# Column rings for the input and output buffers of a grouped 1x1 convolution, and a loop over 64 groups in place of 48

## The chip, the cores and the metric

The kernel runs on one core of one Trainium2 chip. The metric is the device time of one execution in microseconds (us). Where a ratio is given with an interval, it is the record's: the mean time of one kernel's fast runs over the mean of the other's in the same rounds. For the experiments these rounds leave out the profiled run, so it is not quite the ratio of the medians that are quoted.

## The reference, cut to what matters

```python
# x: (1, 512, 512, 192) bf16, w: (1, 1, 4, 48, 48) bf16; k = 1, G = 4, Cg = 48, pad = 0
xg = x.reshape(B, H, W, G, Cg)
out = jnp.einsum('bhwgc,gcd->bhwgd', xg, w[0, 0])      # 1x1 convolution in 4 groups
return out.reshape(B, H, W, C)
```

That is 262,144 pixels with 192 channels. Reading x takes 100.7 MB and writing the output takes 100.7 MB. There is little arithmetic for each byte.

## The kernel before

A "column" is 128 pixels, one on each of the 128 partitions, 384 bytes on each. There are 2,048 columns. They are moved in pieces: 4, 4, 8, 16 columns, then 62 pieces of 32, then 16, 8, 4, 4. A piece of 32 is one DMA of 1.5 MiB, in which each of the 128 partitions has one packet of 12,288 bytes. PE works on "groups" of four columns: six transposes, an eviction by DVE from PSUM to SBUF, six matmuls, and an eviction by ACT to the output buffer. In every third group DVE takes half of that last eviction ("shared" groups).

SP issues the loads, ACT issues the stores. In the kernel before, every piece, however small, holds one of six whole buffers of 32 columns, on either side:

```python
PPC = 32; NBI = 6; NBO = 6; RING = 6
x_sb = [... [128, PPC * C] ... for i in range(NBI)]
o_sb = [... [128, PPC * C] ... for i in range(NBO)]
body = NBI * PPC // 4                    # 48 groups in PE's hardware loop

def shared(g):
    return g % 3 == 1 and g < NG - 3

# SP
for n in range(n_chunks):
    if n >= NBI:
        wq.wait(t_done, chunk_g1[n - NBI])          # transposes of the piece six back
    b = n % NBI
    sp.dma_start(x_sb[b][:, 0:sizes[n] * C], rows_view(xf, n)).then_inc(ld_sem[b], 16)
# ACT, DVE: before the first write into an output buffer
def wait_out_free(wq, n):
    wq.wait(st_sem[n % NBO], 16 * (n // NBO))
# ... (PE, evictions: cut)
```

## Time and profile before

| | before |
|---|---|
| time, median of the first 3 runs | 493.58 us |
| profiled span | 492.4 us |
| bytes moved / mean rate over the span | 201.56 MB / 409 GB/s |
| rate in the middle of the run | 427 to 430 GB/s |
| busy: PE / DVE / ACT | 415 / 358 / 346 us |

These are lines of the page of the kernel before: the busy time of PE, then the span in 40 slices (PE's busy tenths, the DMA engines' mean busy tenths, the rate in GB/s), the queue that brings in instructions in 16 KiB packets, and the chain of waits that ended last, by engine and by line.

```profile
PE 415.0 (84%) x6154; PEld 389.1 (79%) x6154; DVE 358.1 (73%) x683; ACT 345.6 (70%) x513; POOL 1.3 (0%) x8
...
PE   5999999998888888888889888888888888888953
...
DMA  8999999999999999999999999999999999999663
GB/s 294 414 418 425 427 427 429 430 429 429 430 429 429 429 428 427 427 429 427 428 430 429 429 430 430 429 430 427 428 427 429 428 429 429 429 429 427 279 253 143
...
q8 instruction: 7, 0.11, 0.1%
...
DMA 71%; PE 24%; ACT 3%; issue 1%; ACTq 1%; SPq 0%
DMA x_sb<-in_x_dram 71%; PE o_ps L207 13%; PE xT_ps L184 10%; ACT o_sb L274 3%; ACTq L258 1%; SPq L155 0%; SPq L150 0%; ACTq L47 0%
```

DMA is full from the second slice to the 37th, at about 429 GB/s, and no compute engine is. The chain consists mostly of loads of x. So far this looks like a kernel at the bandwidth limit. But the last three slices are far from full, and that calls for a closer look.

The waits of the kernel before (who waited for whom: us in total, times, longest) and then the wait of the load queue on SP:

```profile
DVE xT_sb L242 <- PE xT_ps L184: 109.7, 243, 4.0
ACT o_sb L274 <- PE o_ps L207: 101.6, 169, 7.2
...
PE xT_ps L184 <- DMA x_sb<-in_x_dram: 58.3, 54, 3.2
...
PE o_ps L207 <- ACT o_sb L274: 10.1, 45, 0.4
```

```profile
SPq L155 <- PE xT_ps L184: 427.2, 64, 7.6
```

PE is starved by loads. The queue on SP always waits for transposes: each freed buffer gets its next load at once. No wait for a store is listed. The DMA issues, with the median time from issue to landing:

```profile
x_sb<-in_x_dram SPq DMA_DIRECT2D x62, 1536.0 KB, 39.2
out_dram<-o_sb ACTq DMA_DIRECT2D x62, 1536.0 KB, 31.0
```

A load of 1.5 MiB lands 39.2 us after its issue, though one such piece passes every 7.6 us. About five of the six buffers are thus queued loads. Stretches of the run, with the busy time of each engine, then the granted clock, the DMA engines' share and GB/s:

```profile
core 0: us, PE busy (x) PEld busy (x) DVE busy (x) ACT busy (x) POOL busy (x), PEclk, DMA share, GB/s
135.00:440.00 305.00, 257.58 (x3845) 240.78 (x3843) 224.26 (x428) 215.89 (x322) 0.00 (x0) 1.00 1.01 429
456.00:462.00 6.00, 5.59 (x85) 5.11 (x82) 4.95 (x10) 4.96 (x8) 0.00 (x0) 1.00 0.88 359
462.00:468.00 6.00, 5.06 (x78) 4.85 (x78) 4.34 (x9) 4.00 (x7) 0.00 (x0) 1.00 0.42 178
468.00:474.00 6.00, 4.89 (x75) 4.67 (x76) 4.00 (x8) 4.71 (x7) 0.00 (x0) 1.00 0.59 243
474.00:478.00 4.00, 1.45 (x24) 1.25 (x21) 1.51 (x3) 1.18 (x2) 0.00 (x0) 1.00 0.72 301
...
480.00:482.00 2.00, 0.07 (x1) 0.08 (x2) 0.00 (x0) 0.00 (x0) 0.00 (x0) 0.50 0.06 26
482.00:484.00 2.00, 2.00 (x17) 1.97 (x18) 0.90 (x2) 0.36 (x1) 0.00 (x0) 0.50 0.06 25
```

The share is 1.01 until late and then 0.42 to 0.72, although loads are still outstanding: PE gets its last load at 481.9 us. From 480 to 484 us the share is 0.06, and one engine of 16 would be 0.0625: a single DMA engine is at work. It had no pause earlier: from 60 to 452 us the times of the packets, summed from the packed trace, add up to at least 16.1 engines in every half microsecond (over 16 because packets overlap a little), so no engine stood still. The trace also shows how one engine comes to be left over. Each load and store raises its semaphore 16 times, and the trace has the time of each increment (the load queue holds 1,136 packets of 4 bytes for its 71 DMAs, 16 for each). I read each increment as one engine's share done; the end agrees with that: one store has 15 increments by 472.5 us and the last at 484.2, and from 480 to 484 us one engine is at work. These are the 16 increments, in us from the start, of one load late in the run:

```
406.6 407.0 407.2 407.7 407.8 408.1 408.1 408.1 408.1 408.5 408.9 408.9 408.9 409.5 413.4 424.6
```

Fourteen engines finish their share within 3 us, one is 4 us later, and one is 15 us behind the last of the fourteen. The distance of the last increment from the median is 16.5 us here; for a load at 20 us it was 1.7 us, and it grows steadily. One engine is slower than the others, and this load is not complete until that engine's share is there, at 424.6 us. Of all packets of 12,288 bytes 93% took at most 0.465 us and 5% took 0.475 us or more.

### The profile page before, as it was taken

Reading aid. Unit: us, or ns where it says so; the run is one execution under the profiler, and the core shown is the slowest. Engines: PE = TensorE matmul, PEld = TensorE weight load, DVE = VectorE, ACT = ScalarE, POOL = GpSimd, SP = SyncE. Lnnn points to the kernel's source line nnn. Section 1 sums busy time; section 2 is a strip of 40 time slices with the busy share of each in tenths; the row PEclk is TensorE's granted clock in tenths of the full one; section 3 lists DMA queues with packets and bytes.
Section 4 is the critical chain, followed back from the end, with each engine's and each line's share of the span. In section 5 each row is a group of like instructions: output and inputs, shape, how many; then the busy total and the mean of one; then the engine's idle time right before and its main releaser. Section 6 shows DMA issues by size and latency. Waiting matters only on the chain.

```text
span 492.4 us, 14343 instructions
## 1 busy us (share of the span) xinstructions
PE 415.0 (84%) x6154; PEld 389.1 (79%) x6154; DVE 358.1 (73%) x683; ACT 345.6 (70%) x513; POOL 1.3 (0%) x8
## 2 busy tenths in 40 slices
PE   5999999998888888888889888888888888888953
PEld 5899999887877877878778778787787787877852
DVE  3888888876777777777778777777677777777750
ACT  2788888876766777667767676776776766766752
POOL 1000000000000000000000000000000000000000
PEclk9999999999999999999999999999999999999996
DMA  8999999999999999999999999999999999999663
GB/s 294 414 418 425 427 427 429 430 429 429 430 429 429 429 428 427 427 429 427 428 430 429 429 430 430 429 430 427 428 427 429 428 429 429 429 429 427 279 253 143
DMA packets 20386, 201.56 MB, mean 409 GB/s; under 512 B 2448, under 2 KB 3472, under 8 KB 4496
## 3 DMA queue, kind: packets, MB, share of 16 engines
q1 hardware_dynamic: 10288, 100.69, 48.5%
q10 hardware_dynamic: 10080, 100.67, 48.3%
q8 instruction: 7, 0.11, 0.1%
q14 instruction: 11, 0.09, 0.0%
HBM read 100.68 MB, written 100.66 MB: 409 GB/s over the span
## 4 chain that ended last, share of the span: by engine, by line
DMA 71%; PE 24%; ACT 3%; issue 1%; ACTq 1%; SPq 0%
DMA x_sb<-in_x_dram 71%; PE o_ps L207 13%; PE xT_ps L184 10%; ACT o_sb L274 3%; ACTq L258 1%; SPq L155 0%; SPq L150 0%; ACTq L47 0%
## 5 line engine op out<-in xcount | busy, mean ns | idle before, releaser
L242 DVE COPY xT_sb<-xT_ps 128x768 bf16<-128x768 bf16 x512 | 283.8, 555 | 114.8 <-PE xT_ps L184 109.7
L274 ACT CAST o_sb<-o_ps 128x768 bf16<-128x768 f32 x342 | 267.0, 799 | 107.9 <-PE o_ps L207 101.6
L184 PE MATMUL xT_ps<-ident,x_sb 128*128 128x128 bf16 x3072 | 257.2, 220 | 58.3 <-DMA x_sb<-in_x_dram 58.3
L207 PE MATMUL o_ps<-wt,xT_sb 128*128 128x144 bf16 (+1 forms) x3072 | 297.4, 233 | 10.4 <-ACT o_sb L274 10.1
L184 PEld LDWEIGHTS xT_ps<-ident,x_sb 128*128 128x128 bf16 x3072 | 195.0, 98 | 70.0 <-DMA x_sb<-in_x_dram 68.9
L207 PEld LDWEIGHTS o_ps<-wt,xT_sb 128*128 128x128 bf16 x3072 | 211.5, 98 | 24.5 <-issue 17.7
L271 ACT CAST o_sb<-o_ps 128x384 bf16<-128x384 f32 x170 | 81.6, 480 | 33.3 <-PE o_ps L207 24.0
L248 DVE CAST o_sb<-o_ps 128x384 bf16<-128x384 f32 x170 | 94.2, 554 | 8.1 <-PE o_ps L207 7.0
L237 DVE CAST wt<-o_ps 128x480 bf16<-128x480 f32 x1 | 0.7, 657 | 3.2 <-PE o_ps L167 3.2
L167 PE MATMUL o_ps<-w_sb,esel 48*128 48x48 bf16 x10 | 0.6, 209 | 2.6 <-DMA w_sb<-in_w_dram 2.6
L167 PEld LDWEIGHTS o_ps<-w_sb,esel 48*128 48x128 bf16 x10 | 0.4, 111 | 2.5 <-POOL esel L139 2.5
L274 ACT ACT_TABLE_LOAD x1 | 1.3, 1283 | 0.8 <-PEq L298 0.8
L139 POOL TENSOR_SCALAR_AFFINE_SELECT esel<-esel 48x272 bf16<-48x272 bf16 x1 | 0.4, 406 | 0.0
L136 POOL MEMSET esel<- 48x272 bf16 x1 | 0.3, 318 | 0.3 <-POOLq L298 0.3
L143 POOL TENSOR_SCALAR_AFFINE_SELECT ident<-ident 128x128 bf16<-128x128 bf16 x1 | 0.3, 285 | 0.0
L137 POOL MEMSET ident<- 128x128 bf16 x1 | 0.2, 198 | 0.0
L298 POOL MEMSET const-bfloat16-1.0<- 128x1 bf16 x1 | 0.1, 102 | 0.0
L298 POOL MEMSET const-uint8-127<- 128x1 uint8 x1 | 0.1, 102 | 0.0
L298 POOL MEMSET const-float32-0.0<- 128x1 f32 x1 | 0.1, 98 | 0.3 <-issue 0.3
L298 POOL MEMSET const-float32-1.0<- 128x1 f32 x1 | 0.1, 98 | 0.0
## 6 DMA issues: line engine op xcount, KB each, us to landing
x_sb<-in_x_dram SPq DMA_DIRECT2D x62, 1536.0 KB, 39.2
out_dram<-o_sb ACTq DMA_DIRECT2D x62, 1536.0 KB, 31.0
x_sb<-in_x_dram SPq DMA_DIRECT2D x2, 768.0 KB, 22.1
out_dram<-o_sb ACTq DMA_DIRECT2D x2, 768.0 KB, 11.7
x_sb<-in_x_dram SPq DMA_DIRECT2D x4, 192.0 KB, 15.5
x_sb<-in_x_dram SPq DMA_DIRECT2D x2, 384.0 KB, 19.8
out_dram<-o_sb ACTq DMA_DIRECT2D x4, 192.0 KB, 6.9
out_dram<-o_sb ACTq DMA_DIRECT2D x2, 384.0 KB, 10.2
```

Source lines behind the costliest of these rows:

```text
L136: gp.memset(esel[:], 1.0).then_inc(p0_sem, 1)
L139: gp.affine_select(out=esel[:], in_=esel[:], pattern=[[-1, ECOLS]], compare_op=AluOpType.is_equal, fill=0.0, base=ESHIFT, channel_multipli ...
L167: last = pe.matmul(o_ps[:, NOB - 1, col:col + CG], lhsT=esel[:, s0:s0 + 128], rhs=w_sb[:, g, :], start=True, stop=True, skip_group_check=True)
L184: ins.append(pe.transpose(xT_ps[:, g % NXP, j * 128:(j + 1) * 128], xb[:, col:col + 128], ident[:]))
L207: ins.append(pe.matmul(o_ps[:, v % NOB, c0_:c1_], lhsT=xs[:, j * 128:(j + 1) * 128], rhs=wt[:, WOFF[tc]:WOFF[tc] + (c1_ - c0_)], start=(tc ...
L237: dve.tensor_copy(wt[:], o_ps[:, NOB - 1, 0:WCOLS]).then_inc(wc_sem, 1)
L242: dve.tensor_copy(xT_sb[g % NXP][:], xT_ps[:, g % NXP, 0:2 * UC]).then_inc(e1_sem[g % RING], 1)
L248: dve.tensor_copy(o_sb[n % NBO][:, u * UC:(u + 1) * UC], o_ps[:, v % NOB, 0:UC]).then_inc(d2_sem[g // 3 % 2], 1)
L258: act.dma_start(rows_view(of, n), o_sb[b][:, 0:sizes[n] * C]).then_inc(st_sem[b], 16)
L271: ins = act.copy(ob[:, u * UC:(u + 1) * UC], o_ps[:, v % NOB, 0:UC])
L274: ins = act.copy(dst, o_ps[:, v % NOB:v % NOB + 2, 0:UC])
L298: nc = _bacc.Bacc("TRN2", target_bir_lowering=False, num_devices=1)
```

## The change

The intent is to use the buffers fully. Input and output become one ring of 256 columns each. A piece takes only its own columns, and a load waits only until the transposes have passed the columns that it overwrites. PE's hardware loop then covers a ring, 64 groups in place of 48, and so that this divides evenly, every fourth group is shared in place of every third.

```diff
-PPC = 32
-NBI = 6
-NBO = 6
-RING = 6
+BIG = 32
+RCOLS = 256
+RING = 8
 ...
-    body = NBI * PPC // 4
+    body = RCOLS // 4
 ...
     def shared(g):
-        return g % 3 == 1 and g < NG - 3
+        return g % 4 == 1 and g < NG - 3
 ...
-        x_sb = [... [128, PPC * C] ... for i in range(NBI)]
-        o_sb = [... [128, PPC * C] ... for i in range(NBO)]
+        x_sb = ... [128, RCOLS * C] ...
+        o_sb = ... [128, RCOLS * C] ...
 ...
-        def wait_out_free(wq, n):
-            wq.wait(st_sem[n % NBO], 16 * (n // NBO))
+        def wait_out_free(wq, g):
+            if g >= body:
+                p = store_at[g - body]
+                wq.wait(st_sem[p.key], st_val[p])
 ...
-            for n in range(n_chunks):
-                if n >= NBI:
-                    wq.wait(t_done, chunk_g1[n - NBI])
-                b = n % NBI
-                sp.dma_start(x_sb[b][:, 0:sizes[n] * C], rows_view(xf, n)).then_inc(ld_sem[b], 16)
+            for p in loads:
+                wq.wait(t_done, p.g1 - body)
+                sp.dma_start(ring_view(x_sb, p), rows_view(xf, p)).then_inc(ld_sem[p.key], 16)
 ... (semaphores by piece, indices into the rings: cut)
```

More of the change, by code (lines that the diff above doesn't have):

```diff
@@ L47, in wait, with __init__, plan_pieces @@
         self.eng.wait_ge(sem, val)
-def plan_chunks(npix):
-    assert npix % 512 == 0, "the pixel count must be a multiple of 512"
-    cols = npix // 128
-    head, tail = list(HEAD), list(TAIL)
-    if cols < sum(head) + sum(tail) + PPC:
-        head, tail = [], []
-    mid = cols - sum(head) - sum(tail)
-    first = len(head)
-    full = mid // PPC
-    sizes = head + [PPC] * full
-    if mid % PPC:
-        sizes.append(mid % PPC)
-    return sizes + tail, first, full
+class Piece:
+    def __init__(self, col, size, key):
+        self.col, self.size, self.key = col, size, key
+        self.g0, self.g1 = col // 4, (col + size) // 4
+def plan_pieces(cols, head, tail):
+    sizes = list(head) if cols >= sum(head) + sum(tail) else []
+    last = list(tail) if sizes else []
+    mid = cols - sum(sizes) - sum(last)
+    pieces, c = [], 0
+    for s in sizes + [BIG] * (mid // BIG) + ([mid % BIG] if mid % BIG else []) + last:
+        whole = s == BIG and c % BIG == 0
+        pieces.append(Piece(c, s, ("big", c // BIG % (RCOLS // BIG)) if whole else ("own", len(pieces))))
+        c += s
+    return pieces
 def bass_standalone__grouped__vision_kernel(nc, x, w, out):
@@ L68, in bass_standalone__grouped__vision_kernel @@
     npix = B * H * W_
-    sizes, first_full, n_full = plan_chunks(npix)
-    n_chunks = len(sizes)
+    cols = npix // 128
+    assert npix % 512 == 0, "the pixel count must be a multiple of 512"
+    NG = cols // 4
+    loads = plan_pieces(cols, HEAD, TAIL)
+    stores = plan_pieces(cols, HEAD, TAIL)
+    load_of = {p.g0: p for p in loads}
+    store_at = {g: p for p in stores for g in range(p.g0, p.g1)}
+    store_end = {p.g1 - 1: p for p in stores}
     xf = x.rearrange("b h w c -> (b h w) c")
@@ L75, in bass_standalone__grouped__vision_kernel @@
     wv = w.rearrange("a b g c d -> c (a b g) d")
-    col0, groups, chunk_g0, chunk_g1, c0 = [], [], [], [], 0
-    for n, s in enumerate(sizes):
-        col0.append(c0)
-        c0 += s
-        chunk_g0.append(len(groups))
-        groups += [(n, lg) for lg in range(s // 4)]
-        chunk_g1.append(len(groups))
-    NG = len(groups)
-    body = NBI * PPC // 4
-    assert body % 12 == 0
-    loop_g0 = chunk_g0[first_full]
-    reps = max(0, (n_full * PPC // 4 - LOOK) // body)
+    body = RCOLS // 4
+    assert body % RING == 0 and BIG % 4 == 0 and RCOLS % BIG == 0
+    bigs = [p for p in loads if p.key[0] == "big"]
+    loop_g0 = bigs[0].g0 if bigs else 0
+    reps = max(0, (sum(p.size for p in bigs) // 4 - LOOK) // body)
     loop_g1 = loop_g0 + reps * body
     def shared(g):
-        return g % 3 == 1 and g < NG - 3
+        return g % 4 == 1 and g < NG - 3
     dve_prog = [("wcopy", 0)]
@@ L101, in bass_standalone__grouped__vision_kernel, with rows_view, ring_view @@
             dve_prog.append(("ev2", h))
-    def rows_view(ap, n):
-        s = sizes[n]
-        return ap[128 * col0[n]:128 * (col0[n] + s), :].rearrange("(p i) c -> p (i c)", p=128)
+    def rows_view(ap, p):
+        return ap[128 * p.col:128 * (p.col + p.size), :].rearrange("(p i) c -> p (i c)", p=128)
+    def ring_view(t, p):
+        at = p.col % RCOLS
+        assert at + p.size <= RCOLS
+        return t[:, at * C:(at + p.size) * C]
     with ExitStack() as es:
         block = es.enter_context(nc.Block())
-        x_sb = [es.enter_context(nc.sbuf_tensor(f"x_sb{i}", [128, PPC * C], BF16)) for i in range(NBI)]
-        o_sb = [es.enter_context(nc.sbuf_tensor(f"o_sb{i}", [128, PPC * C], BF16)) for i in range(NBO)]
+        x_sb = es.enter_context(nc.sbuf_tensor("x_sb", [128, RCOLS * C], BF16))
+        o_sb = es.enter_context(nc.sbuf_tensor("o_sb", [128, RCOLS * C], BF16))
         xT_sb = [es.enter_context(nc.sbuf_tensor(f"xT_sb{i}", [128, 2 * UC], BF16)) for i in range(NXP)]
@@ L120, in sem @@
             return es.enter_context(nc.semaphore(name))
-        ld_sem = [sem(f"ld{i}") for i in range(NBI)]
-        st_sem = [sem(f"st{i}") for i in range(NBO)]
+        ld_sem = {k: sem(f"ld_{k[0]}{k[1]}") for k in dict.fromkeys(p.key for p in loads)}
+        st_sem = {k: sem(f"st_{k[0]}{k[1]}") for k in dict.fromkeys(p.key for p in stores)}
+        st_val, seen = {}, {}
+        for p in stores:
+            seen[p.key] = seen.get(p.key, 0) + 16
+            st_val[p] = seen[p.key]
         w_sem, id_sem, e_sem, wb_sem, wc_sem = (sem(s) for s in ("w_sem", "id_sem", "e_sem", "wb_sem", "wc_sem"))
@@ L171, in transposes @@
             def transposes(g):
-                n, lg = groups[g]
                 if g == 0:
                     pe.wait_ge(id_sem, 1)
-                if lg == 0:
-                    pe.wait_ge(ld_sem[n % NBI], 16)
-                xb = x_sb[n % NBI]
+                p = load_of.get(g)
+                if p:
+                    pe.wait_ge(ld_sem[p.key], 16)
                 ins = []
                 for ul in range(2):
-                    u = lg * 2 + ul
+                    u = g % body * 2 + ul
                     for tc in range(3):
@@ L184, in transposes @@
                         ins.append(pe.transpose(xT_ps[:, g % NXP, j * 128:(j + 1) * 128],
-                                                xb[:, col:col + 128], ident[:]))
-                if lg == 0:
-                    ins[1].then_inc(ld_sem[n % NBI], -16)
+                                                x_sb[:, col:col + 128], ident[:]))
+                if p:
+                    ins[1].then_inc(ld_sem[p.key], -16)
                 ins[-1].then_inc(t_done, 1)
@@ L197, in matmuls @@
                     if shared(g - 2):
-                        waited.append(d2_sem[(g - 2) // 3 % 2])
+                        waited.append(d2_sem[(g - 2) // 4 % 2])
                 for s in waited:
@@ L238, in _ @@
                     continue
-                n, lg = groups[g]
                 if op == "ev1":
@@ L243, in _ @@
                 else:
-                    wait_out_free(wq, n)
+                    wait_out_free(wq, g)
                     wq.wait(mm_done, g + 1)
-                    u = lg * 2 + 1
+                    u = g % body * 2 + 1
                     v = 2 * g + 1
-                    dve.tensor_copy(o_sb[n % NBO][:, u * UC:(u + 1) * UC],
-                                    o_ps[:, v % NOB, 0:UC]).then_inc(d2_sem[g // 3 % 2], 1)
+                    dve.tensor_copy(o_sb[:, u * UC:(u + 1) * UC],
+                                    o_ps[:, v % NOB, 0:UC]).then_inc(d2_sem[g // 4 % 2], 1)
         @block.scalar
@@ L254, in _, with store @@
             pending = []
-            def store(n):
-                b = n % NBO
-                act.dma_start(rows_view(of, n), o_sb[b][:, 0:sizes[n] * C]).then_inc(st_sem[b], 16)
+            def store(p):
+                act.dma_start(rows_view(of, p), ring_view(o_sb, p)).then_inc(st_sem[p.key], 16)
             for g in range(NG):
-                n, lg = groups[g]
-                if lg == 0:
-                    wait_out_free(wq, n)
+                wait_out_free(wq, g)
                 wq.wait(mm_done, g + 1)
@@ L267, in _ @@
                 v = 2 * g
-                ob = o_sb[n % NBO]
+                u = g % body * 2
                 if shared(g):
-                    u = lg * 2
-                    ins = act.copy(ob[:, u * UC:(u + 1) * UC], o_ps[:, v % NOB, 0:UC])
+                    ins = act.copy(o_sb[:, u * UC:(u + 1) * UC], o_ps[:, v % NOB, 0:UC])
                 else:
-                    dst = ob[:, lg * 2 * UC:(lg + 1) * 2 * UC].rearrange("p (u c) -> p u c", u=2)
+                    dst = o_sb[:, u * UC:(u + 2) * UC].rearrange("p (u c) -> p u c", u=2)
                     ins = act.copy(dst, o_ps[:, v % NOB:v % NOB + 2, 0:UC])
                 ins.then_inc(fa_sem[g % RING], 1)
-                if g == chunk_g1[n] - 1:
-                    pending.append((n, g + ST_DELAY))
-            for (n, _) in pending:
-                act.wait_ge(fa_sem[(chunk_g1[n] - 1) % RING], 1)
-                store(n)
-            for b in range(NBO):
-                cnt = len(range(b, n_chunks, NBO))
-                if cnt:
-                    wq.wait(st_sem[b], 16 * cnt)
+                if g in store_end:
+                    pending.append((store_end[g], g + ST_DELAY))
+            for (p, _) in pending:
+                act.wait_ge(fa_sem[(p.g1 - 1) % RING], 1)
+                store(p)
+            for p in stores:
+                if st_val[p] == seen[p.key]:
+                    wq.wait(st_sem[p.key], st_val[p])
 _INS = ['x', 'w']
```

## The prediction

> **What bounds the kernel now.** DMA, and not its mean but one of its 16 engines.
> - The slices of the page show 427 to 430 GB/s and a full DMA share from 50 us until three slices before the end. The chain that ended last is 71% loads of x; PE is 84% busy, DVE 73%, ACT 70%. PE is starved by loads 54 times, 58.3 us; no wait for a store appears. In the DMA queue's own waits SP stands 427.2 us on the transposes: each freed input buffer is refilled at once, and that load lands after 39.2 us (median).
> - Each load's semaphore rises 16 times, once per DMA engine. Near 20 us these increments lie within 2.5 us; near 280 us 15 lie within about 6 us, the last 7 to 8 us later; of the load that lands at 468.5 us the median engine was done at 450.2. The last engine's lag behind the median grows steadily, 1.67 us in each 43.9 us: one engine is 3.8% slower. Its 12,288-byte packets take about 0.476 us, most others 0.461.
> - Work of that engine: 62 loads and 62 stores of 8 such packets, 992 x 0.476 = 472 us; small pieces about 16; increments 1; start 2.3. About 491 us (estimate from these); the span is 492.4. From 456 us on the windows show the DMA share fall to 0.42 and less: the others have run out of work. Its last big store lands at 488.0, the small tail stores follow without a gap until 491.8. It is busy throughout.
>
> **What the change does.** The piece sizes stay (4, 4, 8, 16, 62 x 32, 16, 8, 4, 4), so packets and bytes stay. The rings grow from 6 to 8 big pieces, so about two more loads wait in the DMA queue: landing of a big load goes from 39 to about 54 us (estimate: two pieces at 7.3 us). Shared evictions go from every third group to every fourth: ACT gains about 42 x (0.80-0.48) = 14 us (to about 359), DVE loses 42 x 0.554 = 23 us (to about 335), both off the path. A load queue that is never empty gains nothing from depth: critical-path saving about 0.
>
> **The risk: instructions.** PE's loop body grows from 48 to 64 groups, by my count of the built program from 1,202 to 1,602 instructions; the program from 2,038 to 3,238. [...] The trace of before has seven 16 KiB fetches: five in the loop's first pass, none in its nine others, two at the end; the body stayed resident. [...]
>
> **Predicted:** 493.5 us, 491.5 to 495.5. Faster by over 2% 0.02, within 2% 0.88, slower 0.10.
>
> **What would show it.** Right: same rate; DMA share again falls before the end while one engine finishes; its lag again grows near 3.8%; loads land after 50 to 56 us; no wait for stores. Wrong: over 30 fetches of 16 KiB and PE idle at loop starts; or an earlier end of the slow engine, which would mean that depth counts, or that its slowness comes from the buffers' layout.

The sum stands: 472 + 16 + 1 + 2.3, about 491 us for the slow engine, and 493.5 us was forecast for the time.

## The result, and the profile after

| | before | after |
|---|---|---|
| time, median (4 runs each) | 493.42 us | 493.79 us |
| lowest to highest | 493.20 to 493.61 | 492.87 to 494.38 |
| ratio of the fast runs | | 1.0006, 95% interval 0.9989 to 1.0023 |
| last load complete | 481.9 us | 478.6 us |
| last store complete | 491.8 us | 491.3 us |
| busy: PE / DVE / ACT | 415 / 358 / 346 us | 415 / 335 / 362 us |

The time is the same. The lines of the page after that answer to those shown of before:

```profile
PE 414.9 (84%) x6154; PEld 391.2 (80%) x6154; DVE 334.5 (68%) x640; ACT 362.2 (74%) x513; POOL 1.3 (0%) x8
...
PE   5999999999889888898888988978888788898942
...
DMA  8999999999999999999999999999999999999943
GB/s 284 420 427 424 426 425 428 430 428 429 428 428 430 429 428 428 429 428 429 430 430 428 428 429 427 430 428 429 429 430 430 427 427 429 429 426 422 391 179 144
...
q8 instruction: 12, 0.20, 0.1%
...
PE 74%; DMA 11%; another core or an unknown queue 11%; ACT 1%; issue 1%; SPq 0%; ACTq 0%
```

The rates and the fall before the end are the same. The instruction queue has 12 packets of 16 KiB in place of 7. The chain now names PE and "an unknown queue"; these are the pieces of about 1.2 us every 7.6 us where PE stands for a load, and the profile does not name the releaser there. The waits view does name it:

```profile
DVE xT_sb L249 <- PE xT_ps L192: 133.7, 260, 3.8
...
ACT o_sb L274 <- PE o_ps L215: 65.7, 51, 2.4
PE xT_ps L192 <- DMA x_sb<-in_x_dram: 64.5, 53, 2.7
...
PE o_ps L215 <- ACT o_sb L277: 0.9, 4, 0.3
```

```profile
SPq L164 <- PE xT_ps L192: 394.4, 59, 7.3
```

PE is starved as often as before (64.5 us against 58.3). PE's own waits for ACT are gone, 0.9 us against 10.1, and nothing came of it. The issues and the stretches:

```profile
x_sb<-in_x_dram SPq DMA_DIRECT2D x62, 1536.0 KB, 54.9
out_dram<-o_sb ACTq DMA_DIRECT2D x62, 1536.0 KB, 36.8
```

```profile
135.00:440.00 305.00, 256.45 (x3852) 241.22 (x3851) 209.28 (x401) 226.72 (x321) 0.00 (x0) 1.00 1.01 429
456.00:462.00 6.00, 4.79 (x75) 4.46 (x73) 4.05 (x9) 4.12 (x8) 0.00 (x0) 1.00 1.01 424
462.00:468.00 6.00, 6.00 (x95) 5.79 (x93) 4.94 (x11) 5.33 (x9) 0.00 (x0) 1.00 0.86 359
468.00:474.00 6.00, 2.69 (x39) 2.23 (x36) 2.45 (x5) 3.02 (x5) 0.00 (x0) 1.00 0.43 178
474.00:478.00 4.00, 1.47 (x12) 1.13 (x12) 0.56 (x1) 0.80 (x1) 0.00 (x0) 0.59 0.44 184
```

A load now takes 54.9 us to land in place of 39.2. The additional ring space has been filled with loads that wait in the DMA queue, and nothing else. The increments of a load at the same place of the run:

```
405.0 405.4 405.6 406.5 406.8 406.9 407.0 407.1 407.6 407.9 408.0 408.4 409.6 410.1 410.3 421.4
```

One engine is again 11 us behind the rest. Worth a look is how far that engine's progress is the same in both kernels. If the last increments of the stores are put in order, the 20th to the 50th are 7.59 us apart on average before and 7.61 us after. The eighth increments of the loads, which stand for the ordinary engines, are 7.32 us apart in both. The ordinary engines are 4% faster; the slow one sets the time of both kernels.

### The profile page after: what moved, and what is told of

Read it like the earlier page. It is cut to its first block, busy times and chain, and to the rows that moved or that the text cites. A ratio compares the mean times of both kernels' runs of the same rounds, so it can differ in the third digit from the quotient of the medians.

```text
span 491.7 us, 14286 instructions
## 1 busy us (share of the span) xinstructions
PE 414.9 (84%) x6154; PEld 391.2 (80%) x6154; DVE 334.5 (68%) x640; ACT 362.2 (74%) x513; POOL 1.3 (0%) x8
## 3 DMA queue, kind: packets, MB, share of 16 engines
q1 hardware_dynamic: 10288, 100.69, 48.6%
q10 hardware_dynamic: 10080, 100.67, 48.3%
## 4 chain that ended last, share of the span: by engine, by line
PE 74%; DMA 11%; another core or an unknown queue 11%; ACT 1%; issue 1%; SPq 0%; ACTq 0%
PE o_ps L215 41%; PE xT_ps L192 33%; DMA x_sb<-in_x_dram 11%; ACT o_sb L277 1%; ACTq L264 0%; SPq L164 0%; SPq L161 0%
## 5 line engine op out<-in xcount | busy, mean ns | idle before, releaser
L277 ACT CAST o_sb<-o_ps 128x768 bf16<-128x768 f32 x385 | 301.4, 799 | 39.1 <-PE o_ps L215 35.0
L192 PE MATMUL xT_ps<-ident,x_sb 128*128 128x128 bf16 x3072 | 258.1, 221 | 64.7 <-DMA x_sb<-in_x_dram 64.5
L274 ACT CAST o_sb<-o_ps 128x384 bf16<-128x384 f32 x127 | 60.9, 479 | 82.5 <-PE o_ps L215 65.7
L255 DVE CAST o_sb<-o_ps 128x384 bf16<-128x384 f32 x127 | 70.1, 552 | 0.5 <-PE o_ps L215 0.5
## 6 DMA issues: line engine op xcount, KB each, us to landing
x_sb<-in_x_dram SPq DMA_DIRECT2D x62, 1536.0 KB, 54.9
out_dram<-o_sb ACTq DMA_DIRECT2D x62, 1536.0 KB, 36.8
```

Of the source, the lines that this page charges most:

```text
L192: ins.append(pe.transpose(xT_ps[:, g % NXP, j * 128:(j + 1) * 128], x_sb[:, col:col + 128], ident[:]))
L255: dve.tensor_copy(o_sb[:, u * UC:(u + 1) * UC], o_ps[:, v % NOB, 0:UC]).then_inc(d2_sem[g // 4 % 2], 1)
L274: ins = act.copy(o_sb[:, u * UC:(u + 1) * UC], o_ps[:, v % NOB, 0:UC])
L277: ins = act.copy(dst, o_ps[:, v % NOB:v % NOB + 2, 0:UC])
```

## The experiments

Theory A: one DMA engine is slower than the others, it is busy from start to end, and its share of the bytes sets the time; depth of the queue in front of it is worth nothing as long as that queue does not run empty. Rival B: the mean rate of all engines is the bound. Rival C: the deeper ring did gain something, and the shift of evictions to ACT, or the longer loop, gave it back. All kernels gave correct results. They ran on four chips, each time beside runs of the kernel before. All are made from a copy of the changed kernel in which the two ring sizes and the loop length are separate constants, unless said otherwise.

### Input ring of 128 columns

```diff
-XCOLS = 256
+XCOLS = 128
```

> The changed kernel with an input ring of 128 columns, half the depth, four big pieces; output ring as it was. Theory A: the slow engine's queue of loads still never runs empty, so 493.5 within 1 us; big loads land about 26 us after issue in place of 54.9; the lag of the last engine behind the median is capped by the ring, at under 20 us at the end. Rival C (depth of the input ring was worth something, and the change gave it back elsewhere): slower than 496, and slower than before, whose ring has six.

Measured: 494.15 us against 493.01 for the kernel before, ratio 1.0024 (0.9978 to 1.0070). The median landing time of a load:

```profile
x_sb<-in_x_dram SPq DMA_DIRECT2D x62, 1536.0 KB, 24.4
```

The input ring was halved, to less than the kernel before had, and the time is the same within the interval. The last increments of the stores are 7.60 us apart. Depth of the input ring between 128 and 256 columns is worth nothing. Rival C is refuted for the input ring: there was no gain to give back.

### Input ring of 64 columns

```diff
-XCOLS = 256
+XCOLS = 64
```

> The changed kernel with an input ring of 64 columns, two big pieces: where depth should begin to count. Theory A: the slow engine now stands without a load while PE works through a piece (8 groups of 0.81 us, then issue and start), so slower: about 520, 500 to 545. If it is still within 1% of 493.5, the refill after a piece is quicker than I think, and the landings will show it.

Measured: 516.65 and 519.83 us in two runs; two more, of 526 and 531 us, are slow. The mean of the fast two is 5.1% over that of the kernel before (493.26 us). The record's ratio, 1.0606 (1.0510 to 1.0702), comes out for 519.83 and 526.38 us, without the profiled run of 516.65.

```profile
x_sb<-in_x_dram SPq DMA_DIRECT2D x62, 1536.0 KB, 9.7
```

With two pieces the loads land 9.7 us after issue: the queue is now empty again and again. And the signature of the slow engine is gone: late in the run the last increment of a load comes only 2.2 us after the eighth, where it was 15.7 us with 256 columns. All engines now wait for the refill: in 109 of the 784 half microseconds from 60 to 452 us the packets add up to fewer than 16 engines, in the changed kernel in none. The stores' last increments are 7.87 us apart. This is where depth begins to count: between two and four pieces, far below both kernels.

### The shift of evictions alone

The kernel before, with one part of the change:

```diff
     def shared(g):
-        return g % 3 == 1 and g < NG - 3
+        return g % 4 == 1 and g < NG - 3
 ... (and g // 3 % 2 becomes g // 4 % 2 for the semaphores)
```

> The kernel before with one part of the change alone: every fourth group shared between ACT and DVE in place of every third; rings of six buffers stay. Theory A and Rival C differ: A says the shift of 14 us to ACT is off the path, 493.5 within 1 us. Rival C (the deeper ring gained something, the shift to ACT gave it back) says slower than 496.

Measured: 493.34 us against 493.13, ratio 1.0004 (0.9978 to 1.0031). It explains part of the profile after, though: its last load is complete at 478.1 us (before 481.9, after 478.6) and its stores take 35.8 us to land (before 31.0, after 36.8). PE's wait for ACT is 0.7 us (before 10.1, after 0.9). These three differences come from the evictions, not from the rings, and none moves the end.

### Output ring of 128 columns

```diff
-OCOLS = 256
+OCOLS = 128
```

> The changed kernel with an output ring of 128 columns, input ring 256. Stores take 36.8 us to land at one each 7.6 us, so nearly 5 are outstanding on the slow engine; a ring of four makes ACT and DVE wait for stores, for the first time. Theory A: the slow engine still has loads queued whenever PE is held up, so it stays busy: 493.5 to 497, with waits for stores in the trace and fewer outstanding. If over 500, depth of the output ring does matter and the queue of loads alone does not keep the engine busy.

Measured: 493.77 us against 493.13, ratio 1.0010 (0.9980 to 1.0041). The waits of this run:

```profile
ACT o_sb L284 <- DMA out_dram<-o_sb: 74.8, 56, 1.4
PE o_ps L220 <- ACT o_sb L284: 69.6, 60, 1.3
...
DVE o_sb L260 <- DMA out_dram<-o_sb: 24.7, 54, 0.5
...
PE xT_ps L197 <- DMA x_sb<-in_x_dram: 2.1, 2, 1.5
```

ACT and DVE now wait about 100 us in all for stores, and PE 70 us for ACT, where the kernel before had no wait for a store and 10.1 us of PE for ACT. The time is the same, and the last increments of the stores are 7.59 us apart. Such waits look grave in a profile; here they only replace PE's wait for loads, 2.1 us in this run and 64.5 in the changed kernel.

### A loop of 128 groups

```diff
-LOOPG = 64
+LOOPG = 128
```

> The changed kernel with PE's hardware loop over 128 groups in place of 64, rings and pieces unchanged: about 3,200 instructions a pass[...]. Expected: 16 KiB fetches rise from 12 to about 48 (0.8 MB). Time by theory A: unchanged at 493 to 495 if they are spread over the engines or fall on a fast one with room (20 us of it); 505 to 510 if all fall on one fast engine that then becomes the slowest; over 515 if they fall on the slow one. If fetches stay at 12 to 15, a long loop isn't refetched and my risk was empty.

Measured: 494.53 us against 493.01, ratio 1.0032 (0.9988 to 1.0076). The instruction queue:

```profile
q8 instruction: 53, 0.87, 0.7%
```

There are 53 fetches, one about every 9 us through the whole run. They did not fall on the slow engine: the stores' last increments are 7.62 us apart, as ever, while the eighth increments of the loads went from 7.32 to 7.45 us. So other engines carried this and became slower, and the slow engine's lag at the end shrank from 15.7 to 9.0 us. It was several of them: in the load that is complete at 460.2 us ten of the 15 ordinary increments come 3.9 to 10.0 us after the first, while in the changed kernel at the same place all 15 lie within 5.2 us. PE stood still 13.1 us at its transposes in seven waits for nothing that the profile shows (0.2 us in one wait in the changed kernel), and it waited less for loads, 47.7 us in place of 64.5. The time did not follow them. Ordinary engines had room for these 0.87 MB.

### Extra work on some of the engines

The most direct test of theory A is to give work to some engines and not to others. How many engines carry a DMA I read from its increments, one for each; which ones can't be read, since the trace doesn't name a packet's engine. My plans for these runs assumed an order in which partitions fall on the engines, and with it a number for the slow one. No trace or run shows that order, so engines are counted here, not numbered. Two runs were made to find which engine is slow.

In the first, four stores are cut in two, of 120 and 8 partitions, meant to leave one engine out of them:

```diff
+OFF = (14, 28, 42, 56)
+PARTS = (0, 120, 128)
-                act.dma_start(rows_view(of, p), ring_view(o_sb, p, OCOLS)).then_inc(st_sem[p.key], 16)
+                for a, b in zip(cut, cut[1:]):          # cut = PARTS in these four stores
+                    act.dma_start(to[a:b, :], fro[a:b, :]).then_inc(st_sem[p.key], 16)
```

> The changed kernel, but four of the 70 stores (numbers 14, 28, 42, 56) go out as two DMAs, of partitions 0 to 119 and 120 to 127. [...] Theory A (one slow engine is busy throughout and ends the kernel): [...] it has 4 x 8 x 0.476 = 15 us less to do, and the time falls to 478 to 483 us; if it is another one it gets up to 4 packets more, and the time is 493 to 496. [...] Rival B (the mean rate of 430 GB/s is the bound, all engines together): the bytes are the same, so 493.5 to 495 whichever engine it is.

The first case of theory A is that the slow engine carries nothing of the four; "another one" is any engine that carries some of them. Both are my estimates.

Measured: 497.51 us against 493.01, ratio 1.0104 (1.0037 to 1.0171). So these stores were not taken off the slow engine. The store queue has 10,108 packets in place of 10,080 in the changed kernel, 28 more: 23 increments for each cut store in place of 16. Each cut store has two late increments, for example 228.2 and 230.0 us where the others end at 223.5: the slow engine is in both parts. The time is 1.5 us over the range expected for that case; eight packets of the stores took over 1.2 us (up to 2.3), which none does in the changed kernel, where the longest takes 0.87. The second run cuts six stores in three:

```diff
+CUTS = {34 + 3 * s: (0, s, 112 + s, 128) for s in range(2, 8)}
```

> A diagnosis, not a timing. The changed kernel with six of the stores (numbers 40, 43, 46, 49, 52, 55) cut into three DMAs of s, 112 and 16-s partitions, s = 2 to 7[...]. [...] because both DMAs of a cut store had one late increment. Now two increments are late [...], all six stores have two late ones. Time within 1% of 493.5.

That two increments are late in all six stores is what I guessed.

Measured: 509.18 us in a single run of unknown state; the time is far off what was expected. In all six stores two increments stood out. I took that for the answer, and this was a misreading: a third one, if there is one, is hidden among those of the second slowest engine. What can be read is the time from the slow engine's increment of the store before to its increment of the 112 partitions: 6.9 and 6.7 us at s = 2 and 3, about seven eighths of the 7.6 us that this engine takes for a store, but 10.0, 9.6, 9.5 and 9.9 us at s = 4 to 7, which is more. By inference the slow engine carried a packet of the first part from s = 4 on; which engine that makes it is not shown.

Before I had seen that, I had loaded 20 stores in the same way:

```diff
+CUTS = {n: (0, 120, 128) for n in range(6, 66, 3)}
```

> The changed kernel with 20 of the stores sent as 120 + 8 partitions: [...] all bytes as before. Theory A: 20 x 0.476 = 9.5 us more on the slow engine, so 502 to 505 us. Rival B (mean rate of all engines): bytes the same, 493.5 to 495.

Theory A's 20 packets are one more in each cut store, an estimate from the run of four cut stores, where the slow engine was in both parts.

Measured: 521.79 us in the one fast run, the other three at 532 to 539; the fast run is 5.8% over the mean of the kernel before (493.41 us). The record's ratio, 1.0873 (1.0803 to 1.0942), comes out for the other three, without the profiled run. Even 5.8% is much more than either theory says, and the rate falls in the whole run:

```profile
GB/s 301 415 423 427 414 427 419 428 425 407 418 405 427 417 413 410 412 422 409 395 414 408 408 402 410 387 395 393 392 400 398 391 407 388 377 347 329 291 206 164
```

The reason is in the packets: 171 packets of the stores took 1.2 us or more (up to 2.8), against none in the changed kernel, where the longest takes 0.87. What lengthened them is not shown. The experiment doesn't tell A from B, since it made the transfers themselves slower.

The next three runs went to one chip. The first has extra loads of 49 partitions into a tile that nothing reads, four times, meant to go past the slow engine (and the output ring of 128 columns, which costs nothing, to make room):

```diff
+EXTRA = (12, 26, 40, 54)
+EXTRA_P = 49
+                if loads.index(p) in EXTRA:
+                    i = EXTRA.index(loads.index(p))
+                    sp.dma_start(extra[0:EXTRA_P, i * BIG * C:(i + 1) * BIG * C],
+                                 rows_view(xf, p)[0:EXTRA_P, :]).then_inc(ex_sem[i], 16)
```

> The changed kernel (output ring 128, which the last run showed to be free, to make room) with four extra loads of 49 partitions x 12 KiB into a tile that nothing reads; results stay right. [...] 28 packets, 13 us more for each of seven engines, none for the slow one[...]. Theory A: these engines have 13 to 17 us to spare, so 493 to 496 us. Rival B (mean rate): 2.4 MB more at 430 GB/s, 5.6 us more, 499.

The same with 63 partitions, meant to reach the slow engine as well:

```diff
-EXTRA_P = 49
+EXTRA_P = 63
```

> The same with 63 partitions in place of 49[...]. Theory A: 28 x 0.476 = 13.3 us more, 505 to 509 us. Rival B: 3.1 MB more, 7.2 us, 500.5; the two kernels then differ by 1.6 us only.

Measured: 510.85 us with 49 partitions and 512.69 us with 63, against 493.55; ratios 1.0337 (1.0308 to 1.0366) and 1.0383 (1.0360 to 1.0406). The run with 49 partitions contradicts the 493 to 496 us that theory A gave for engines other than the slow one, and it is the choice of engines that was wrong. The load queue has 10,512 packets in place of 10,288 in the changed kernel: 4 x 49 packets of data and 4 x 7 increments more, seven engines for each extra load. The last of the extra loads shows the slow one among them. Its eight recorded increments (the first comes 36.6 us before the rest; I read it as the remainder of the 16 for which the kernel waits) are:

```
341.8 378.4 380.3 380.5 383.0 383.0 385.4 402.9
```

The last of the seven is 17 us behind the others: the slow engine is one of the seven, and it did get the extra work. What was expected for that, 13.3 us for 28 packets of 0.476 us (seven for each of the seven engines, four times; for 63 partitions an estimate by the same count), is most of the 17.3 and 19.1 us measured. The traces show a part of the rest. The profiled execution with 49 partitions was one of the two shortest, 507.60 us, only 14.1 us over the median of the kernel before. In the one with 63 (511.78 us) the last load is complete at 501.6 us and the slow engine's last store of 32 columns at 502.5 (in the trace of before: 481.9 and 488.0). From 502 to 505 us the DMA share is 0.03 and PE is busy 2.8 of 3.0 us: nearly all DMA engines waited for the last stores, a time that the kernel before filled with stores still queued. Rival B is refuted by the size: 1.2% more bytes cost 3.4% of the time. At full rate they would cost 5.6 us.

With two extra loads of 51 partitions the same weight of extra work was meant for three engines only, without the slow one:

```diff
-EXTRA = (12, 26, 40, 54)
-EXTRA_P = 49
+EXTRA = (12, 33)
+EXTRA_P = 51
+EXTRA_W = (6144, 4096)            # elements of each row: 12 KiB, then 8 KiB
```

> The run with extra loads again[...]: two extra loads of 51 partitions (17 packets for each of three engines, rows of 12 KiB and then of 8 KiB), 13 us more on each[...]. [...] Theory A: nothing of this falls on the slow engine, the three have that much to spare, so 493 to 497 us, and none of the three increments of an extra load is far behind the other two. [...] Rival B (mean rate): 1.0 MB more, 2.4 us, 496.

Measured: 495.41 us against 493.10, ratio 1.0047 (1.0033 to 1.0061), in five rounds. The recorded increments of the two extra loads, in each of which three follow the first by over 50 us, so that I count three engines:

```
 19.6  71.7  72.9  72.9
175.5 238.0 239.1 239.6
```

No one trails: the slow engine is not among these three. Had the run cost over 10 us all the same, theory A would have fallen. The three loaded engines fell 23 to 27 us behind the ordinary ones in the loads, further than the slow engine (a load's increments: 397.4 at first, 400.2 the eighth, 405.8 the twelfth, then 422.2, 423.1, 425.0, 427.0 for the last four; the first of these four is the slow engine's, by its pace of 7.6 us a load over the seven loads before, where the other three keep 7.3). So 13 us on three engines without the slow one cost 2.3 us, and 13 us on seven engines with it cost 17.3. Here are PE's busy slices and the rate of this run, and then the rate of the run on seven engines:

```profile
PE   6999786989888888887199999788787887877993
...
GB/s 299 418 418 426 428 416 428 429 429 429 428 428 429 429 429 429 429 428 428 430 429 429 428 429 429 427 429 429 429 429 429 428 428 429 429 423 321 289 287 264
```

```profile
GB/s 305 420 419 425 427 424 429 430 428 429 428 429 428 427 428 428 432 426 427 432 428 421 429 428 428 429 429 427 429 426 423 428 333 400 426 411 297 205 261 257
```

On three engines PE stands nearly still in slice 20, after the second extra load (complete at 239.6 us), by my reading because the next piece lacks the shares of three engines; and it still costs only 2.3 us. In that stretch the slow engine's stores came later (four took it 30.5 us from 186.7 to 217.2, but 32.4 us from 247.3 to 279.7), yet it did not run dry: from 236 to 268 us the packets add up to at least 16.1 engines in every half microsecond, so it moved loads while PE had no stores to give. Where the 2.3 us were lost is not shown. This run alone can't tell A from B, since B says 2.4 us. Together with the run on seven engines it does, though the two ran on different chips, each beside the kernel before.

### Work past the slow engine

```diff
+CUTS = {n: (0, 120, 128) for n in (14, 28, 42, 56)}
+            gp.dma_start(turn[0:8, 0:64], xf[0:8, 0:64]).then_inc(tn_sem[0], 16)
+            for i, p in enumerate(q for n, q in enumerate(stores) if n in CUTS):
+                gp.wait_ge(mm_done, p.g1 + ST_DELAY)
+                for a, b, x in zip(cut, cut[1:], (st_sem[p.key], gp_sem[p.key[1]])):
+                    gp.dma_start(to[a:b, :], fro[a:b, :]).then_inc(x, 16)
+                gp.dma_start(turn[0:9, (i + 1) * 64:(i + 2) * 64], xf[0:9, 0:64]).then_inc(tn_sem[i + 1], 16)
 ... (ACT leaves these four stores out)
```

> The changed kernel, with four stores (numbers 14, 28, 42, 56) issued from GpSimd as 120 + 8 partitions. [...] If so the slow engine has 4 x 7 packets less, 13 us: theory A says 480 to 486 us, faster than both kernels. [...] were seen to take 1.2 to 2.8 us a packet in the cut stores, which can eat the gain. Rival B: 493.5 or more in any case.

"If so" means: if each of the four stores leaves the slow engine one packet in place of eight. The small loads into `turn` were meant to bring that about; that they can is not shown. What "were seen to take 1.2 to 2.8 us" is packets of the cut stores, in the runs above.

Measured: 498.95 us against 493.55, ratio 1.0092 (1.0065 to 1.0119). There was no gain, and twelve 12 KiB packets of ACT's other stores took 1.3 to 2.4 us at the times of two of these four, as was seen beside the other cut stores. Of the 12 KiB packets of these four stores themselves 42 took over 1.2 us, up to 3.2. On which engines they ran is not shown, so whether these stores went past the slow engine is open. No version was found that beats the two kernels.

## Why the prediction was right

- **"DMA, and not its mean but one of its 16 engines."** Right. In the kernel before, the changed one, and the variants with other rings, other evictions and a longer loop, the slow engine passes a store every 7.59 to 7.62 us, and the time is 493 to 495 us in all of them. When ordinary engines got more to do (the loop of 128 groups, the extra loads on three engines) the time rose by 0.3 to 0.5%; when the slow one was among those that got it (extra loads on seven engines), by 3.4%. That the slow engine is busy throughout is shown from 60 to 452 us, where the packets leave no engine idle, and from 480 to 484 us, where one engine alone is at work; for the time between it is inferred from the even pace, since the trace doesn't name a packet's engine.
- **"A load queue that is never empty gains nothing from depth."** Right. The input ring can go down to 128 columns, and the output ring as well. At 64 columns the queue runs empty and the time rises by 5%.
- **Landing of a load 39 to about 54 us.** Measured 54.9: more pieces in the queue, the same pace, so a longer wait for each.
- **ACT 359, DVE 335 us, both off the path.** Measured 362 and 335; the shift alone gave a ratio of 1.0004.
- **Instructions: the longer loop is fetched once.** So it was forecast, and the argument for it, a size of PE's instruction memory, is not shown. Measured: 12 blocks of 16 KiB fetched in place of seven, of which seven in the first pass of the loop (18.9 to 69.7 us), none in its other passes, five after it (433.2 to 469.8 us).
- **The cost if it were fetched again** was mis-sized. With a loop of about 3,200 instructions (my count) 53 blocks were fetched, and it cost 1.5 us by the medians, with an interval of the ratio that includes 1. The step that failed is my assumption that all fetches would fall on one engine and make it the slowest: they fell on several ordinary ones, which went from 7.32 to 7.45 us a load and stayed below the slow engine's 7.62. As the changed loop was not fetched again, the forecast time didn't rest on this term.
- The last load is complete 3.3 us earlier than before. I hadn't foreseen it; it comes from the evictions and is worth nothing, since the slow engine's stores end at 491.3 us in place of 491.8.

What stays open: why this engine is slower, which one it is and whether it is the same on every chip, the part of the cost of the extra loads (17.3 and 19.1 us) that neither the slow engine's 13.3 us of packets nor the idle end of the run accounts for, and the 2.3 us of the run on three engines.

## What to carry to other kernels

When DMA is the bound, look at the 16 increments of one transfer before you look at the mean rate: where one engine trailed by more and more, in the kernel before by 1.7 us at 20 us and 16.5 at 425, its share of the bytes was the time, and depth, balance between compute engines and shorter waits elsewhere were worth nothing (493 to 495 us in all those runs). The queue needed only as much depth as keeps it from running empty, here between two and four pieces (516.65 us and more with two, 494.15 with four); what came on top showed as a longer time to landing, 24.4, 39.2 and 54.9 us with four, six and eight pieces. And before cutting a transfer to unload one engine, check what a cut costs: stores over other than 128 partitions had packets of up to 2.8 us in place of 0.46.
